# A new table of planner thresholds for the exponential-bound attention stage of an adaLN transformer block

## The chip, the cores and the metric

The kernel runs on one core of a Trainium2 chip. The metric is the device time of one execution in microseconds (us); the median of the runs is compared. Engines are named PE (TensorE matmuls; PEld are its weight loads), DVE (VectorE), ACT (ScalarE), POOL (GpSimd) and SP (SyncE, which issues most transfers).

## The reference

One transformer block with adaptive layer norm, batch 1, 2048 tokens, width 640, in bf16. Six vectors of 640 come from the conditioning row `c`; then attention with 32 heads of 20 and a gated feed-forward layer of width 1536 without an activation.

```python
mod = (silu(c) @ w_mod)                       # six vectors: sa, ca, ga, sb, cb, gb
h = layernorm(x) * (1 + ca) + sa
q, k, v = split(h @ wqkv)                     # 32 heads, 20 wide
p = softmax(q @ k.T * 20 ** -0.5)             # 32 x 2048 x 2048 exponentials
x = x + ga * ((p @ v) @ wo)
h = layernorm(x) * (1 + cb) + sb
x = x + gb * (((h @ w_gate) * (h @ w_up)) @ w_down)
```

## The kernel before

**Units.** Queries are cut into seven chunks (one of 512, six of 256); heads go in eight groups of four, one head on each 32-row strip of PE's array. An item is a chunk and a group. Its work is cut into units: one strip, key tiles of 128 rows, 512 columns of scores in one PSUM bank. For most units PE computes scores (line 1824), ACT takes the exponential of two units at once, 128 x 1024, from PSUM into two of the 16 slots of `PP` (line 2801, 798 instructions), and PE multiplies by the values (PV, line 2504), which frees the slots. 452 units, in 113 groups of four, take another way: DVE turns scores into integers (line 1851), splits them into two factors (lines 1887 and 1895), and multiplies one of them (line 1892 on DVE, or four pieces on POOL, line 1907); both factors then go through PV.

**Work around it.** The rest of the block is cut into rounds ("X work"), one PSUM bank each: transposes of the normalised tiles (line 1390) and their evacuation (lines 1396 and 1398), projections to K, Q and V (lines 1429, 1493 and, with the column-tiled helper, 1233), the output projection, the second layer norm, gate, up and down projections (lines 1233 and 1229). A chunk's output projection and feed-forward layer run while the exponentials of the next chunk go on; what is left of the last two chunks runs after the last exponential, and that is called the tail here. The tiles `hprodt` belong to the last chunk but one, `hprodc` to the last.

**The planner.** The order on each engine is not written by hand. While the program is built, a planner (`Sched`) steps through a modelled time, and at each step gives every free engine its next task; the lists that come out are the instruction order of the engines, which run them strictly in order and wait on semaphores. PE's choice is made in `pick_pe`: scores first when a bank pair is free (`visit`), then X work or PV by thresholds.

The thresholds are module globals. `stage(it)` sets them from a base, then from `STAGE[it]` for the item whose PV is under way, then from `SEGT[segment]`, where a segment is `SEG = 8` exponentials:

```python
    def stage(it):
        globals().update(base)
        globals().update(STAGE.get(it, {}))
        globals().update(SEGT.get(seg[0], {}))

    def segment():
        while sc.progress >= SEG * (seg[0] + 1):
            seg[0] += 1
            stage(st_pv["item"])
```

`sc.progress` counts the exponentials and ends at 798, so segments run from 0 to 99. Segment 0 holds from the first instruction on.

What the thresholds do:

- `XG`: X rounds have a gate, a number of exponentials; a round may start when its gate is not over `progress + XG`.
- `XFIRST`: X work is taken ahead of PV while at least so many pairs of `PP` slots are free. `XCONT`: the same for a round that has been begun.
- `PVMIN`, `PVMAX`, `PVCAP`, `PVTOL`: how many PV units must be ready, how many are taken at once, how late the next scores may get for them. `PV_OPEN`, `PV_KEEP`: how many items PV may be open in, and how many banks it must leave free.
- `HOLD`: PE waits for scores that are so many ns away. `X_HALF`, `X_LATE`: when a matmul of a round is cut in two to let scores in.
- `EAGER`, `D_LATE`, `D_RES`: how early or late scores for the DVE way are made, and when a bank is kept for them.
- `LKTOL`: how long a DVE instruction may be kept waiting by POOL's products. `XBACK`: how many of POOL's pieces may be outstanding when DVE takes a product itself.
- `STEAL_GAP`: ACT takes over an evacuation from DVE when nothing of its own is due within so many ns. In `steal` this ends at 66.2 us of planned time, and begins again only past the last exponential.
- `TPRIO`, `XDPRIO`: priorities, read when the tasks of the DVE way are created, which is before the first call of `stage`.

Of the kernel before, what the change touches and what calls it, by code (L numbers as in the profile page):

```python
# [775 lines left out]

SEG = 8
SEGT = {
    1: {"PVTOL": 152.9, "XFIRST": 5},
    2: {"EAGER": 5},  # L780
    3: {"LKTOL": 409.9, "PVMAX": 4},
    5: {"HOLD": 18.3, "X_HALF": 186.9},
    6: {"PVCAP": 10, "PVTOL": 128.9, "XCONT": 2, "XDPRIO": 1.229},
# [5 lines left out]
    13: {"HOLD": 90.7, "XG": 9},
    14: {"PV_OPEN": 1, "XBACK": 2, "XCONT": 6, "XG": -2},  # L790
    16: {"EAGER": 11, "PVTOL": 31.8, "XCONT": 4},
    17: {"D_RES": 22, "PVTOL": 373.5, "STEAL_GAP": 131.6},
    18: {"D_RES": 22, "LKTOL": 422.8, "PVMAX": 8, "PVMIN": 7, "PVTOL": 373.5, "STEAL_GAP": 131.6},
    20: {"PVTOL": 309.1, "XCONT": 0, "XG": 9},
    21: {"HOLD": 53.2, "PVMIN": 3, "PVTOL": 86.9},
    22: {"D_RES": 49, "PVCAP": 6},
    24: {"HOLD": 52.6},
    25: {"D_LATE": 13, "PV_KEEP": 3},
    26: {"EAGER": 12, "STEAL_GAP": 219.1, "XCONT": 5},
    27: {"XBACK": 2, "XG": -5},  # L800
    28: {"XCONT": 4},
    29: {"D_RES": 18, "EAGER": 15, "HOLD": 1.1, "XFIRST": 2},
    31: {"PVMAX": 6, "XDPRIO": 0.985},
    33: {"XCONT": 2, "XG": 3},
    34: {"HOLD": 14.4, "PVTOL": 187.4},
    36: {"D_LATE": 18, "EAGER": 8, "TPRIO": 0.426},
    37: {"D_LATE": 18, "EAGER": 8, "TPRIO": 0.426, "XCONT": 3},
    38: {"D_LATE": 18, "EAGER": 8, "HOLD": 14.3, "LKTOL": 40.3, "TPRIO": 0.723, "XCONT": 3, "XG": 4},
    39: {"D_LATE": 18, "EAGER": 8, "LKTOL": 40.3, "PV_OPEN": 3, "TPRIO": 0.723, "XCONT": 3, "XG": 4},
    40: {"EAGER": 6, "PVMIN": 6},  # L810
    41: {"EAGER": 3, "XFIRST": 3},
    42: {"EAGER": 4, "PV_OPEN": 1},
    43: {"XG": 14, "X_LATE": 69.8},
    44: {"EAGER": 14, "XFIRST": 5},
    45: {"EAGER": 14, "XFIRST": 5},
    46: {"D_LATE": 22, "D_RES": 20, "HOLD": 148.8},
    47: {"D_LATE": 22, "HOLD": 148.8, "PVMAX": 3, "XG": -2},
    48: {"EAGER": 2},
    49: {"EAGER": 5, "PVCAP": 15, "PV_KEEP": 4, "X_LATE": -212.0},
    50: {"EAGER": 11, "LKTOL": 38.6, "PVCAP": 15, "PV_KEEP": 4, "XDPRIO": 0.893, "X_LATE": -212.0},  # L820
    51: {"PVMIN": 5, "XBACK": 3, "XDPRIO": 0.768},
    52: {"HOLD": 97.6, "PV_OPEN": 3},
    53: {"XBACK": 2},
    54: {"HOLD": 148.1},
    55: {"PVMAX": 9, "PVMIN": 7, "PVTOL": 138.0, "TPRIO": 0.846},
    56: {"HOLD": 2.5, "PVMAX": 9, "PVMIN": 7, "PVTOL": 138.0, "PV_OPEN": 3, "TPRIO": 0.846, "X_HALF": 88.4, "X_LATE": -103.8},
    57: {"HOLD": 2.5, "PVMAX": 9, "PVMIN": 7, "PVTOL": 138.0, "PV_OPEN": 3, "TPRIO": 0.846, "X_HALF": 88.4, "X_LATE": -103.8},
    58: {"HOLD": 59.0},
    59: {"PVMAX": 4, "PV_KEEP": 1},
    60: {"PVCAP": 9, "XCONT": 2},  # L830
    61: {"LKTOL": 659.0, "PV_KEEP": 2},
    62: {"HOLD": 161.6, "XDPRIO": 1.236, "X_LATE": 20.3},
    64: {"PVCAP": 11, "PVMIN": 7, "XG": 10},
    65: {"EAGER": 10, "PVMIN": 3, "TPRIO": 0.795},
    66: {"HOLD": 0, "X_HALF": 144.4},
    67: {"EAGER": 14, "PVMAX": 13, "PV_KEEP": 2},
    68: {"EAGER": 5, "PVMAX": 13, "PV_KEEP": 2, "XG": -6, "X_LATE": 52.7},
    69: {"X_LATE": 187.0},
    70: {"HOLD": 9.6, "X_HALF": 37.7},
    72: {"HOLD": 202.6, "PV_OPEN": 3, "XDPRIO": 1.458},  # L840
    74: {"PVMIN": 5, "PV_KEEP": 4, "XG": 6},
    75: {"EAGER": 6, "HOLD": 0, "PVMIN": 2},
    76: {"LKTOL": 45.1, "PVMIN": 5, "PVTOL": 121.2},
    77: {"LKTOL": 45.1, "PVMIN": 5, "PVTOL": 121.2},
    81: {"X_LATE": 207.1},
    82: {"D_LATE": 37, "EAGER": 13, "XDPRIO": 0.618, "XFIRST": 2, "X_LATE": 207.1},
    83: {"XDPRIO": 1.036, "XFIRST": 4},
    84: {"STEAL_GAP": 206.3, "XCONT": 5},
    85: {"D_LATE": 5, "LKTOL": 647.8, "PV_KEEP": 4, "STEAL_GAP": 206.3, "XCONT": 5, "XG": 11},
    86: {"PVTOL": 117.5, "XBACK": 1, "XCONT": 2, "XFIRST": 4},  # L850
    87: {"PVMIN": 3, "PVTOL": 378.0, "XBACK": 0, "XCONT": 4},
    88: {"HOLD": 193.8},
    89: {"EAGER": 4, "HOLD": 193.8, "PVCAP": 17, "XG": -4},
    91: {"PVMIN": 3, "PV_KEEP": 2, "X_HALF": 0.7},
    93: {"PVCAP": 7, "PVMAX": 9, "X_LATE": -4.5},
    94: {"HOLD": 60.0, "PVCAP": 15, "PVMAX": 9, "X_LATE": -4.5},
    95: {"HOLD": 197.8, "PVCAP": 15, "PVMAX": 5, "PV_KEEP": 1, "X_LATE": -4.5},
    96: {"HOLD": 197.8, "PVCAP": 15, "PVMAX": 5, "PV_KEEP": 1, "XCONT": 5, "X_LATE": -4.5},
# [2214 lines left out]
```

## Time and profile before

| what | value |
|---|---|
| median of 3 runs | 795.71 us (795.64 to 795.74) |
| the profiled execution | 795.55 us, span 793.8 us |
| granted TensorE clock in the profile | 1.000 |
| busy in the span | PE 783.9, ACT 752.4, DVE 711.2, POOL 358.1 us |
| exponentials | 798, from 16.74 us to 762.01 us |

Times in the profile count from the start of the span. Busy time of PE is modelled and overlaps, and an ACT instruction is recorded from its start to its last write, so that neighbours overlap; what an engine waited for tells more than its share. A row of the timeline gives start, length, engine, line, operation, tiles, shapes and count, and in brackets the idle time before it with what ended it. A row of the waits gives the waiting engine and line, the one waited for, the sum in us, the times and the longest.

### The profile page before, as it was taken

How to read it: one execution, taken by the hardware profiler on the slowest of the kernel's cores; microseconds unless marked ns; L12 is line 12 of the kernel's file. 1: busy time of each engine (PE TensorE's matmuls, PEld its weight loads, DVE VectorE, ACT ScalarE, POOL GpSimd, SP SyncE). 2: the span in 40 equal slices, each digit the busy share in tenths (PEclk: the TensorE clock that was granted, in tenths of full speed). 3: DMA queues.
4: the chain of work that ended last, by engine and by line, in shares of the span. 5: the costliest groups of instructions: out<-in, count | busy, mean ns of one | idle time of the engine just before them, and what ended most of it. 6: DMA issues, size and time to landing. Idle time of an engine off the chain costs nothing.

```text
span 793.8 us, 36358 instructions
## 1 busy us (share of the span) xinstructions
PE 783.9 (99%) x16556; PEld 378.9 (48%) x16556; DVE 711.2 (90%) x1317; ACT 752.4 (95%) x837; POOL 358.1 (45%) x372
## 2 busy tenths in 40 slices
PE   8999999999999999999999999999999999999998
PEld 4433433333244444445455555545554455545567
DVE  7889888988999999989999989988999999898974
ACT  6999899999999999999999999999999999999941
POOL 3334646142466555444453536336355445353510
PEclk9999999999999999999999999999999999999999
DMA  9633222102351622110033305131430146214600
GB/s 301 218 111 98 63 61 61 60 25 71 107 130 43 198 46 52 44 36 20 11 94 69 70 19 117 40 68 36 102 86 21 33 105 135 62 38 91 137 20 19
DMA packets 146090, 61.88 MB, mean 78 GB/s; under 512 B 113215, under 2 KB 145935, under 8 KB 145935
## 3 DMA queue, kind: packets, MB, share of 16 engines
q1 hardware_dynamic: 145007, 58.40, 28.5%
q8 instruction: 130, 2.13, 1.1%
q10 hardware_dynamic: 928, 1.15, 0.4%
q14 instruction: 25, 0.20, 0.1%
HBM read 50.53 MB, written 8.99 MB: 75 GB/s over the span
## 4 chain that ended last, share of the span: by engine, by line
ACT 63%; PE 33%; DVE 3%; DMA 0%; issue 0%; SPq 0%
ACT PP L2801 63%; PE ps_all L1824 10%; PE ps_all L1233 8%; PE ps_all L2504 7%; PE ps_all L1493 3%; PE ps_all L1229 3%; DVE DB L1851 1%; DMA x<-in_A_x_dram 0%; PE ps_all L1429 0%; ACT xn L1300 0%; PE ps_all L1390 0%; PE ps_all L2148 0%; DVE DSS L1887 0%; PE ps_all L2966 0%; DVE st L2106 0%
## 5 line engine op out<-in xcount | busy, mean ns | idle before, releaser
L2801 ACT ACTIVATE PP<-ps_all 128x1024 bf16<-128x1024 f32 x798 | 734.6, 1169 | 4.8 <-PE ps_all L2504 2.6
L1907 POOL TENSOR_TENSOR DSS<-DB,DSS 128x512 bf16<-128x512 bf16 x252 | 287.0, 1159 | 309.3 <-DVE DSS L1895 227.1
L1851 DVE TENSOR_SCALAR DB<-ps_all 128x512 int16<-128x512 f32 x452 | 301.9, 683 | 40.3 <-PE ps_all L1824 38.4
L1824 PE MATMUL ps_all<-QT,KT 32*128 32x256 bf16 (+2 forms) x3648 | 315.3, 286 | 3.0 <-ACT PP L2801 1.0
L1824 PEld LDWEIGHTS ps_all<-QT,KT 32*128 32x128 bf16 x3648 | 92.2, 92 | 203.7 <-ACT PP L2801 182.5
L2504 PE MATMUL ps_all<-PP,Vf 128*32 128x256 bf16 (+4 forms) x2844 | 157.6, 290 | 0.3 <-DVE Vf L1593 0.2
L1233 PE MATMUL ps_all<-h2T,stg 128*32 128x256 bf16 (+2 forms) x2784 | 119.6, 279 | 0.2 <-DVE DB L1851 0.2
L2504 PE MATMUL ps_all<-DSS,Vf 128*32 128x256 bf16 (+1 forms) x1608 | 93.3, 288 | 0.1
L2504 PEld LDWEIGHTS ps_all<-PP,Vf 128*32 128x32 bf16 (+1 forms) x2844 | 58.6, 95 | 65.3 <-issue 56.7
L1887 DVE TENSOR_SCALAR DSS<-DB 128x2048 int16<-128x2048 int16 x113 | 79.2, 701 | 0.7
L1895 DVE TENSOR_SCALAR DSS<-DB 128x2048 int16<-128x2048 int16 x113 | 78.3, 693 | 1.2 <-PE ps_all L2504 1.2
L1233 PEld LDWEIGHTS ps_all<-h2T,stg 128*32 128x32 bf16 x2784 | 59.1, 96 | 36.3 <-issue 30.6
L1233 PE MATMUL ps_all<-wd,hprod 128*32 128x320 bf16 (+1 forms) x1364 | 62.3, 280 | 0.2
L1892 DVE TENSOR_TENSOR DSS<-DB,DSS 128x2048 bf16<-128x2048 bf16 x50 | 61.8, 1238 | 0.1
L2504 PEld LDWEIGHTS ps_all<-DSS,Vf 128*32 128x32 bf16 (+1 forms) x1608 | 40.5, 96 | 16.7 <-issue 9.0
L1989 POOL TENSOR_TENSOR OTn<-OT,invT 128x160 bf16<-128x160 f32 (+1 forms) x44 | 26.5, 622 | 44.3 <-DVE invT L1984 44.3
L1233 PEld LDWEIGHTS ps_all<-wd,hprod 128*32 128x32 bf16 x1364 | 31.0, 96 | 15.1 <-issue 11.4
L1233 PE MATMUL ps_all<-wV,hT 128*32 128x160 bf16 x1280 | 36.1, 234 | 0.0
L1493 PE MATMUL ps_all<-hT,wk 128*32 128x512 bf16 (+1 forms) x360 | 32.4, 382 | 0.0
L1493 PE MATMUL ps_all<-hT,wq 128*32 128x512 bf16 x375 | 31.3, 383 | 0.0
L1233 PE MATMUL ps_all<-wo,Ocp 128*32 128x320 bf16 (+1 forms) x656 | 30.2, 282 | 0.3 <-DVE DB L1851 0.2
L1233 PEld LDWEIGHTS ps_all<-wV,hT 128*32 128x32 bf16 x1280 | 23.4, 96 | 13.0 <-issue 8.3
(128 smaller groups left out, 513.8 us busy)
## 6 DMA issues: line engine op xcount, KB each, us to landing
stg<-in_B_w_gate_dram SPq DMA_DIRECT2D x74, 160.0 KB, 2.5
stg<-in_B_w_up_dram SPq DMA_DIRECT2D x74, 160.0 KB, 2.8
KT<-k_rows SPq DMA_DIRECT2D x28, 128.0 KB
QT<-q_rows SPq DMA_DIRECT2D x48, 64.0 KB, 2.1
wm<-in_w_mod_dram SPq DMA_DIRECT2D x3, 800.0 KB, 6.2
x<-in_A_x_dram SPq DMA_DIRECT2D x7, 320.0 KB
k_rows<-KPA SPq DMA_DIRECT2D x16, 128.0 KB, 2.7
wd<-in_B_w_down_dram SPq DMA_DIRECT2D x1, 1920.0 KB
```

The costliest lines, as they stand in the source:

```text
L1229: return lambda e, b: e.matmul(ps[:, b, c0:c0 + n], lhs(), rhs(), start=st, stop=sp)
L1233: return lambda e, b: e.matmul(ps[32 * x:32 * x + 32, b, c0 + o:c0 + o + w], lhs()[:, 32 * x:32 * x + 32], rhs() if w == n else rhs()[:, o ...
L1493: f = [lambda e, b_, k=k, x=x: e.matmul(ps[x:x + min(32, w - x), b_, :], wx[:, k, r0 + x:r0 + min(x + 32, w)], hT[tc][:, k, :], tile_posit ...
L1824: ems.append(lambda e, i=i, kt=kt: e.matmul(dstf()[:, i * u.n:(i + 1) * u.n], KT[32 * u.s:32 * u.s + 32, u.j, kt * 128:(kt + 1) * 128], QT ...
L1851: return e.tensor_scalar(DBl[st_["slot"]][:, x * 512:(x + 1) * 512], bank(cell["b"]), EBIAS, 0.0, op0=ALU.add, op1=ALU.max)
L1887: return e.tensor_scalar(DSl[st_["ss"][0]][:, :], DBl[st_["slot"]][:, :], 0x7F, 0x3F00, op0=ALU.bitwise_and, op1=ALU.bitwise_or)
L1892: return e.tensor_tensor(d, DBl[st_["slot"]][:, :].bitcast(BF16), d, ALU.mult)
L1895: return e.tensor_scalar(DSl[st_["ss"][1]][:, :], DBl[st_["slot"]][:, :], 0x7F80, 2, op0=ALU.bitwise_and, op1=ALU.bitwise_or)
L1907: return e.tensor_tensor(d, DBl[st_["slot"]][:, x * w:x * w + w].bitcast(BF16), d, ALU.mult)
L1989: return lambda e: e.tensor_tensor(OTn[:, g0:g0 + gn, DH * (j + x):DH * (j + x) + DH, :].rearrange("p b c r -> p b r c"), OT[:, nq_ * x:nq ...
L2504: ems.append(lambda e, i=i, kt=kt, stt=stt, stp=stp: e.matmul(ps[32 * s:32 * s + mc, binfo["bank"], c0:c0 + u.n], Vf[:, (kt * H + 4 * u.j ...
L2801: return e.activation(o, ps[:, b0:b0 + nu, :], AFT.Exp, scale=ESCALE)
```

## The change

All entries of `SEGT` are replaced. The functions, the stage table, the base values and the work to be done stay as they are, so the instructions are the same kinds in another order on each engine's list; an evacuation may change between DVE and ACT, a product between DVE and POOL. The old table has 83 entries between segments 1 and 99, the new one has one for each segment from 0 to 100. Cut to the first segments and a few later ones:

```diff
 SEGT = {
-    1: {"PVTOL": 152.9, "XFIRST": 5},
-    2: {"EAGER": 5},
-    3: {"LKTOL": 409.9, "PVMAX": 4},
-    5: {"HOLD": 18.3, "X_HALF": 186.9},
-    6: {"PVCAP": 10, "PVTOL": 128.9, "XCONT": 2, "XDPRIO": 1.229},
-    7: {"D_LATE": 18, "D_RES": 15, "HOLD": 49.8, "PVCAP": 18},
-    9: {"HOLD": 75.5, "XBACK": 2},
-    10: {"EAGER": 14, "HOLD": 75.5, "TPRIO": 0.516, "XBACK": 0},
-    11: {"EAGER": 11, "PVTOL": 20.3, "XCONT": 3, "XG": -8},
...
-    97: {"PVMAX": 10},
-    98: {"X_LATE": -11.0},
-    99: {"PVMAX": 3, "XCONT": 3, "X_HALF": 4.5},
+    0: {"D_LATE": 16, "EAGER": 13, "STEAL_GAP": 188.8, "XG": 12},
+    1: {"D_LATE": 16, "EAGER": 1, "PVMAX": 7, "PVMIN": 7, "STEAL_GAP": 188.8, "XG": 12, "X_HALF": 129.4},
+    2: {"EAGER": 2, "PVCAP": 11},
+    3: {"EAGER": 2, "HOLD": 0, "PVCAP": 11},
+    4: {"EAGER": 2, "PVCAP": 11, "PVMAX": 11, "STEAL_GAP": 187.3, "XFIRST": 2},
+    5: {"EAGER": 2, "HOLD": 127.5, "LKTOL": 736.9, "PVCAP": 11, "PVMAX": 11, "STEAL_GAP": 187.3, "XFIRST": 2},
+    6: {"D_LATE": 23, "PVCAP": 6, "XCONT": 2},
+    7: {"D_LATE": 23, "PVCAP": 6, "XFIRST": 3},
+    8: {"D_LATE": 23, "PVCAP": 6, "PV_OPEN": 2, "XFIRST": 3, "X_LATE": 54.3},
+    9: {"HOLD": 4.3, "PV_OPEN": 1, "STEAL_GAP": 199.2},
+    10: {"LKTOL": 704.1, "PV_KEEP": 4, "XCONT": 3},
+    11: {"D_RES": 60, "PVCAP": 13, "PVTOL": 181.6, "PV_KEEP": 4, "XCONT": 3},
...
+    97: {"D_LATE": 40, "HOLD": 0},
+    98: {"PV_KEEP": 1},
+    99: {"EAGER": 10, "PVCAP": 10, "PVMIN": 3, "XFIRST": 3},
+    100: {"D_LATE": 12, "EAGER": 10, "LKTOL": 106.2, "PVCAP": 10, "PVMIN": 3, "XFIRST": 3, "X_LATE": 159.4},
 }
```

Stage 0, which holds with segment 0, has `"STEAL_GAP": 83.514`; the base value of `XG` and of `XFIRST` is 0.

More of the change, by code (lines that the diff above doesn't have):

```diff
@@ L778 @@
 SEGT = {
-    1: {"PVTOL": 152.9, "XFIRST": 5},
-    2: {"EAGER": 5},
-    3: {"LKTOL": 409.9, "PVMAX": 4},
-    5: {"HOLD": 18.3, "X_HALF": 186.9},
-    6: {"PVCAP": 10, "PVTOL": 128.9, "XCONT": 2, "XDPRIO": 1.229},
-    7: {"D_LATE": 18, "D_RES": 15, "HOLD": 49.8, "PVCAP": 18},
-    9: {"HOLD": 75.5, "XBACK": 2},
-    10: {"EAGER": 14, "HOLD": 75.5, "TPRIO": 0.516, "XBACK": 0},
-    11: {"EAGER": 11, "PVTOL": 20.3, "XCONT": 3, "XG": -8},
-    12: {"EAGER": 6, "PVTOL": 25.5, "XDPRIO": 1.926},
@@ L789 @@
[L789 to L858, printed above, removed]
@@ new lines @@
+    6: {"D_LATE": 23, "PVCAP": 6, "XCONT": 2},
[4 more added lines that the diff above has]
+    11: {"D_RES": 60, "PVCAP": 13, "PVTOL": 181.6, "PV_KEEP": 4, "XCONT": 3},
+    12: {"PVMAX": 4, "PV_OPEN": 3, "X_HALF": 148.6},
+    13: {"PVTOL": 12.4, "XBACK": 0, "XFIRST": 0},
+    14: {"PVTOL": 12.4, "XBACK": 0, "XCONT": 3, "XFIRST": 0},
@@ new lines @@
+    15: {"EAGER": 11},
+    16: {"XCONT": 4},
+    17: {"EAGER": 6, "HOLD": 0, "PV_KEEP": 1, "XFIRST": 6},
+    18: {"D_LATE": 37, "EAGER": 6, "HOLD": 0, "PV_KEEP": 1, "XCONT": 6, "XFIRST": 6},
+    19: {"D_LATE": 16, "XG": -7},
+    20: {"X_LATE": 190.1},
+    21: {"D_LATE": 31, "PVMIN": 2, "X_LATE": 43.2},
+    22: {"D_LATE": 31, "PVCAP": 6, "PVMIN": 2, "X_LATE": 43.2},
+    23: {"HOLD": 114.5},
+    24: {"PVMIN": 7, "PV_OPEN": 2, "XG": -1, "X_LATE": -155.2},
+    25: {"PVMAX": 5},
+    26: {"D_RES": 23, "LKTOL": 416.7, "XFIRST": 6, "X_HALF": 187.2},
@@ new lines @@
+    27: {"EAGER": 2, "XCONT": 0, "XG": 11},
+    28: {"PVMIN": 7},
+    29: {"PVCAP": 5, "PVMIN": 7},
+    30: {"PVCAP": 5, "PVMIN": 7, "XBACK": 0, "XFIRST": 2},
+    31: {"HOLD": 0, "PVCAP": 5, "PVMIN": 7, "XBACK": 0, "XFIRST": 2, "X_HALF": 0},
+    32: {"D_RES": 43, "XCONT": 3},
+    33: {"PVCAP": 5, "XCONT": 7, "X_HALF": 46.2},
+    34: {"PVCAP": 5, "XCONT": 2, "X_HALF": 46.2},
+    35: {"HOLD": 77.2, "PVTOL": 293.3},
+    36: {"X_LATE": 223},
+    37: {"EAGER": 7, "PVCAP": 14, "PV_KEEP": 3, "STEAL_GAP": 43},
@@ new lines @@
+    38: {"PVMIN": 7},
+    39: {"PVMIN": 6, "X_HALF": 105.7},
+    40: {"EAGER": 16, "XFIRST": 6, "X_LATE": 184.1},
+    41: {"PV_KEEP": 2, "XG": 2, "X_HALF": 107.4},
+    42: {"HOLD": 0, "LKTOL": 335.1, "XCONT": 4},
+    43: {"EAGER": 12, "HOLD": 0, "LKTOL": 335.1, "XCONT": 4},
+    44: {"HOLD": 0, "XFIRST": 6},
+    45: {"HOLD": 200.5, "PVMIN": 7, "XG": -2},
+    46: {"HOLD": 63.7, "PVMAX": 13, "PVMIN": 7, "PVTOL": 185.4, "STEAL_GAP": 22.7, "XG": -2},
+    47: {"XG": 4},
+    48: {"PVMAX": 3, "XFIRST": 4, "XG": -3},
@@ new lines @@
+    49: {"PVTOL": 50.4},
+    50: {"X_HALF": 87.8},
+    51: {"PVMIN": 4, "XCONT": 5, "XG": 12},
+    52: {"PVTOL": 371.2, "PV_KEEP": 2, "XCONT": 4},
+    53: {"PVCAP": 11, "X_LATE": 21.6},
+    54: {"LKTOL": 739.9, "PVMIN": 6, "XFIRST": 0},
+    55: {"LKTOL": 739.9, "PVMIN": 6, "XFIRST": 2},
+    56: {"LKTOL": 739.9, "PVMIN": 6, "PVTOL": 330.9, "XCONT": 0, "XFIRST": 4},
+    57: {"PV_OPEN": 1, "XG": 13},
+    58: {"PVMAX": 7, "PVMIN": 6},
+    59: {"EAGER": 15, "PV_KEEP": 2, "STEAL_GAP": 53.4},
@@ new lines @@
+    60: {"EAGER": 15, "PV_KEEP": 2, "STEAL_GAP": 53.4, "XCONT": 0},
+    61: {"HOLD": 115.6, "PVMAX": 3},
+    62: {"D_RES": 21, "EAGER": 2, "HOLD": 0},
+    63: {"LKTOL": 695.8, "XCONT": 5},
+    64: {"PVCAP": 15, "PV_KEEP": 2, "X_LATE": -22.1},
+    65: {"PVCAP": 15, "PVMAX": 2, "PVMIN": 1, "PV_KEEP": 2, "X_LATE": -22.1},
+    66: {"D_RES": 33, "XFIRST": 5},
+    67: {"HOLD": 94.3, "LKTOL": 8.3, "PV_OPEN": 3, "XG": 13},
+    68: {"PVTOL": 121.8, "PV_KEEP": 2},
+    69: {"D_LATE": 26, "PVCAP": 5, "X_LATE": -228.8},
@@ new lines @@
+    70: {"EAGER": 16, "STEAL_GAP": 0},
+    71: {"EAGER": 16, "STEAL_GAP": 0, "XFIRST": 3, "X_LATE": -97.6},
+    72: {"D_LATE": 17, "EAGER": 16, "PV_OPEN": 1, "STEAL_GAP": 0, "XFIRST": 3, "X_HALF": 76.8, "X_LATE": -97.6},
+    73: {"D_LATE": 17, "EAGER": 16, "PVMAX": 2, "PV_OPEN": 1, "STEAL_GAP": 0, "XFIRST": 0, "X_HALF": 76.8, "X_LATE": -97.6},
+    74: {"EAGER": 6, "HOLD": 40.1, "X_LATE": 77.7},
+    75: {"LKTOL": 30.4, "XCONT": 3},
+    76: {"PV_OPEN": 3, "STEAL_GAP": 0},
+    77: {"PVMAX": 2, "STEAL_GAP": 19.5, "XCONT": 7},
@@ new lines @@
+    78: {"EAGER": 3, "XCONT": 3},
+    79: {"EAGER": 3, "HOLD": 90.6, "XCONT": 7},
+    80: {"PV_KEEP": 4, "XFIRST": 6, "X_LATE": -104.5},
+    81: {"EAGER": 6, "PV_KEEP": 4, "STEAL_GAP": 5.3, "X_LATE": -104.5},
+    82: {"EAGER": 11, "PVCAP": 10, "PV_OPEN": 3, "XCONT": 6},
+    83: {"XCONT": 6, "X_LATE": -223.3},
+    84: {"PVTOL": 177.6},
+    85: {"HOLD": 203.7, "PVMAX": 7, "PVTOL": 177.6, "XBACK": 1},
+    86: {"PV_OPEN": 1, "X_LATE": 136.6},
+    87: {"XCONT": 4},
+    88: {"D_LATE": 4, "PVCAP": 19, "X_HALF": 106.8, "X_LATE": -29.9},
@@ new lines @@
+    89: {"X_HALF": 8},
+    90: {"D_LATE": 9, "EAGER": 5, "STEAL_GAP": 43.9, "X_HALF": 8},
+    91: {"PV_OPEN": 3, "X_LATE": 136.5},
+    92: {"XBACK": 2, "XFIRST": 6},
+    93: {"XCONT": 0, "X_LATE": -34.4},
+    94: {"EAGER": 14, "XCONT": 0, "X_LATE": -34.4},
+    95: {"D_RES": 38, "EAGER": 14, "XCONT": 0, "X_LATE": 150.7},
+    96: {"EAGER": 4, "X_HALF": 138.5},
+    97: {"D_LATE": 40, "HOLD": 0},
+    98: {"PV_KEEP": 1},
+    99: {"EAGER": 10, "PVCAP": 10, "PVMIN": 3, "XFIRST": 3},
+    100: {"D_LATE": 12, "EAGER": 10, "LKTOL": 106.2, "PVCAP": 10, "PVMIN": 3, "XFIRST": 3, "X_LATE": 159.4},
```

## The prediction

> **What bounds the kernel now.** I read the page first: busy shares and the chain that ended last.
>
> ```profile
> span 793.8 us, 36358 instructions
> PE 783.9 (99%) x16556; PEld 378.9 (48%) x16556; DVE 711.2 (90%) x1317; ACT 752.4 (95%) x837; POOL 358.1 (45%) x372
> ...
> ACT 63%; PE 33%; DVE 3%; DMA 0%; issue 0%; SPq 0%
> ...
> L2801 ACT ACTIVATE PP<-ps_all 128x1024 bf16<-128x1024 f32 x798 | 734.6, 1169 | 4.8 <-PE ps_all L2504 2.6
> L1907 POOL TENSOR_TENSOR DSS<-DB,DSS 128x512 bf16<-128x512 bf16 x252 | 287.0, 1159 | 309.3 <-DVE DSS L1895 227.1
> L1892 DVE TENSOR_TENSOR DSS<-DB,DSS 128x2048 bf16<-128x2048 bf16 x50 | 61.8, 1238 | 0.1
> ```
>
> PE looks fuller than ACT, so the waits decide which of them waits for the other.
>
> ```profile
> PEld ps_all L1824 <- ACT PP L2801: 182.5, 667, 0.5
> ...
> ACT PP L2801 <- PE ps_all L2504: 2.6, 3, 1.9
> ...
> ACT PP L2801 <- PE ps_all L1824: 1.7, 6, 0.6
> ```
>
> The weight loads ahead of scores waited 182.5 us for exponentials to free their PSUM banks, in 667 waits; the exponentials waited 4.3 us for PE. ACT sets the pace from the first exponential to the last. What stands between the exponentials is in ACT's timeline, in three windows (the second starts where the 81st is running).
>
> ```profile
> 16.74 7.40 ACT L2801 ACTIVATE PP<-ps_all 128x1024 bf16<-128x1024 f32 x8
> 24.23 0.59 ACT L1503 CAST KPA<-ps_all 128x512 bf16<-128x512 f32 x1
> 25.31 0.59 ACT L1443 CAST KT<-ps_all 128x512 bf16<-128x512 f32 x1 [0.49 <-PE ps_all L1429]
> 25.79 0.50 ACT L1594 CAST Vf<-ps_all 128x160 bf16<-128x160 f32 x2
> 26.53 7.44 ACT L2801 ACTIVATE PP<-ps_all 128x1024 bf16<-128x1024 f32 x8 [0.23 <-PE ps_all L1824]
> 33.83 2.29 ACT L1396 ACTIVATE hT<-ps_all,mcol 128x512 bf16<-128x512 bf16 x3
> 36.98 0.78 ACT L1396 ACTIVATE hT<-ps_all,mcol 128x512 bf16<-128x512 bf16 x1 [0.86 <-PE ps_all L1390]
> 37.84 42.27 ACT L2801 ACTIVATE PP<-ps_all 128x1024 bf16<-128x1024 f32 x46
> 80.28 6.52 ACT L2801 ACTIVATE PP<-ps_all 128x1024 bf16<-128x1024 f32 x7 [0.16 <-PE ps_all L1824]
> 88.67 1.94 ACT L2801 ACTIVATE PP<-ps_all 128x1024 bf16<-128x1024 f32 x2 [1.87 <-PE ps_all L2504]
> ...
> 99.64 144.45 ACT L2801 ACTIVATE PP<-ps_all 128x1024 bf16<-128x1024 f32 x157
> 244.27 88.18 ACT L2801 ACTIVATE PP<-ps_all 128x1024 bf16<-128x1024 f32 x95 [0.18 <-PE ps_all L1824]
> 333.05 88.11 ACT L2801 ACTIVATE PP<-ps_all 128x1024 bf16<-128x1024 f32 x96 [0.59 <-PE ps_all L1824]
> ...
> 754.32 7.69 ACT L2801 ACTIVATE PP<-ps_all 128x1024 bf16<-128x1024 f32 x8
> ```
>
> The time falls into three parts: 16.74 us up to the first exponential, 745.27 us from there to the end of the last (754.32 + 7.69 = 762.01), and 31.8 us of tail. One exponential is recorded with 1169 ns on the mean, but they overlap. Eight of them in 7.44 us make (7.44 - 1.17) / 7 = 0.90 us from start to start, and I take that as the floor: 797 x 0.90 + 1.17 = 718.5 us. So 745.3 - 718.5 = 26.8 us lie above the floor, and only an order can move those. The first 80 exponentials took 99.64 - 16.74 = 82.9 us, 10.9 over 80 x 0.90; the other 718 took 662.4 us, or (662.4 - 1.17) / 717 = 0.922 each, 15.9 over.
>
> The Trainium skill, "ScalarE: Activation LUTs", section "What ACT_TABLE_LOAD costs", prices an ACTIVATE with immediate scale and bias at 186 ns plus 0.833 ns an element, less about 93 ns of overlap when they follow back to back. By it, 1024 columns would come every 186 + 853 - 93 = 946 ns, the stretch could not be under 755 us, and no order could win anything in it; this trace's 745.27 us disagrees, and the measurement decides.
>
> **The change, part by part.** Every instruction that does the model's work stays: 798 exponentials, 113 groups on the VectorE route (50 second products on VectorE, 252 / 4 = 63 on GpSimd). The planner reads other thresholds from the start on, so the order differs on every queue. What may change its engine is an evacuation taken over by ACT, and a second product: 1238 ns of VectorE or 4 x 1159 ns of GpSimd, which is 45% busy; this lies beside the exponentials and I price it at nothing as long as the 16 slots of PP do not fill up. Loads on SyncE's queue move with the staging buffers that PE frees; I price that at nothing while other rounds lie between a load and its use. Without that cover a load that lands late would hold PE, which runs its list in order, and with it the scores behind: a block like that in (c).
>
> Some entries cannot act. The counter does not reach segment 100. ACT takes work over only before 66 us or past the last exponential, so STEAL_GAP of segments 9 to 90 is dead. TPRIO and XDPRIO, which the old table sets, were read when tasks were made, before any segment.
>
> (a) *Up to the first exponential, segment 0.* The old table has no segment 0. STEAL_GAP rises from the stage's 83.514 to 188.8 and XG from 0 to 12. Nothing shown excludes either sign; a block of 0.86 us of filler matmuls lies on the chain here.
>
> ```profile
> 10.62 1.12 PE ps_all L1390 x20
> 11.74 0.86 PE ps_all L2994 x4
> 12.61 1.29 PE ps_all L1429 x20
> ```
>
> I bound it by one such block each way, -0.9 to +0.9, and take 0: the fillers stand where normalised tiles are awaited.
>
> (b) *Exponentials 9 and 17, segments 0 to 2.* Between the first eight and the ninth lie 26.53 - 24.14 = 2.39 us, before the seventeenth 37.84 - 33.97 = 3.87: evacuations on ACT, and waits for PE. The ninth needs the second key tile, the seventeenth the third, so some of this stays in any order. The larger STEAL_GAP lets ACT take over less, but the same 0.6 to 0.8 us then falls on VectorE. Ends: -1.6, the three waits of 0.49, 0.23 and 0.86; +1.4, two more evacuations at 0.6 to 0.8. I take -0.3.
>
> (c) *The block at 80 to 91 us, segments 8 and 9.* The exponential at 88.67 waited 1.87 us for L2504, a PV matmul: PP was full, and PV could not drain it. All-engine timeline of that place:
>
> ```profile
> 87.21 0.53 PE L1233 MATMUL ps_all<-wV,hT 128*32 128x160 bf16 x20
> ...
> 87.57 0.85 PE L1233 MATMUL ps_all<-wmb,SCb 128*32 128x320 bf16 x20
> 87.80 0.33 DVE L1593 CAST Vf<-ps_all 128x160 bf16<-128x160 f32 x1
> 88.17 0.10 PEld L2504 LDWEIGHTS ps_all<-PP,Vf 128*32 128x32 bf16 x3
> ```
>
> A V projection, its evacuation at 87.80, and PV right after: PV waited for values, which came late among the projections. The new table brings such work forward ahead of this place (XG 12 in segments 0 and 1; XFIRST 2 in 4 and 5, 3 in 7 and 8, which takes projections before PV while that many pairs of slots are free); the old one has XFIRST only in segment 1, at 5. Ends: -1.9, the whole wait; +1.9, a second of the same kind, since XFIRST also holds PV back. I take -1.2, nearer the gain.
>
> (d) *The other 718 exponentials, segments 10 to 99.* No single wait exceeds 0.6 us. Were all as in the quiet row of 96, (88.11 - 1.17) / 95 = 0.915, the gain would be 717 x 0.007 = 5.0; as in the row of 95, 0.926, the loss 2.9. Most of this is scattered, 0.18 us for eight, in both rows. I take -0.4.
>
> (e) *The tail.* PE ends it, and part of its work there could have come earlier. The window past the last exponential for line 1233 alone (length, then PE's busy time with its count, then the weight loads'), and rows of the chain:
>
> ```profile
> 762.00:793.80 31.80, 4.76 (x124) 3.04 (x124) 1.00 0.07 23
> ...
> 764.26 1.09 PE ps_all L1233 x28
> ...
> 769.17 1.61 PE ps_all L1233 x44
> ...
> 773.34 17.79 PE ps_all L1229 x261
> ```
>
> 124 down-projection matmuls of the chunk before run past the last exponential, 0.038 us each. All done earlier: -4.8.
>
> ```profile
> L1233 PE MATMUL ps_all<-wd,hprodt 128*32 128x320 bf16 x192 | 8.4, 301 | 0.0
> ```
>
> Of that kind there are 192 in all, so 68 were done earlier; all of them late: +2.6. I take -0.3, since in the tail they also stand where PE would wait for the normalisation of the last tile.
>
> Sum: 0 - 0.3 - 1.2 - 0.4 - 0.3 = -2.2 us. The profiled execution took 795.55 us (span 793.8 and 1.75 around it), so 793.35; the median of the runs is 0.16 above it, so 793.5.
>
> **The rivals.** *No change, 795.7.* What the first 80 exponentials gain is given back: the same VectorE work then falls into less time, and VectorE, for which POOL waits above, is nearly full in later stretches.
>
> ```profile
> 230.00:340.00 110.00, 105.84 (x188) 1.00 0.30 79
> 480.00:520.00 40.00, 39.15 (x70) 1.00 0.31 69
> 560.00:660.00 100.00, 96.93 (x168) 1.00 0.29 67
> ```
>
> 96% to 98% here. A backlog ends as full PP slots and one or two waits like (c). Against it: these stretches hold no such wait now. That the new table moves only what is scattered comes to the same time.
>
> *Slower, 798.3.* More of the chunk's down-projections end behind the last exponential: (e) at its upper end, +2.6, with the rest as before. It decides from 1.6 / 0.038 = 42 more matmuls on. For it: thresholds that keep ACT fed defer other work, and its price shows only at the end. Against: PE has slack enough before (the 182.5 us of waits).
>
> *The floor by the skill's rule.* With exponentials at 946 ns nothing in (b), (c) and (d) can be won, and prologue and tail stay: 795.7. As the trace stands 10 us under that floor I leave it 2 in 100.
>
> **How the numbers follow.** Forecast (faster) 48 in 100, no change 28, floor 2, slower 22. A change within 0.2%, 1.6 us, is about what a measurement here cannot tell from none. The range takes half of the summed lower ends of (b) to (e), -13.3 / 2 = -6.6 (they do not fall together), which gives 789.1, and for the upper end the slower case less 0.5, since other parts still gain: 797.8. The forecast's own range is 789.1 to 794.1.
>
> **What would show it.** Right: in ACT's timeline the block near 88 us is gone or under 1 us; the 81st exponential starts before 98.5; the last ends near 760; the tail is 31 to 32 us. (b) wrong: the sum of the two gaps, 6.3 us, moves by over 1.5. (c) wrong: a wait for L2504 of more than 1 us anywhere. (d): the mean over 718 leaves 0.915 to 0.926. (e): the count of 124 moves by over 40. Most of all a new wait of ACT of 2 us or more after 100 us would make the prediction wrong.

## The result and the profile after

The changed kernel takes 788.72 us, median of 4 runs (788.61 to 788.79), beside 795.73 (795.64 to 795.82) before: 7.0 us less, ratio 0.9912 [0.9895, 0.9929]. It is faster, as forecast, but by three times the forecast of 2.2 us; the time lies 0.4 us under the lower end of the range. The profiled execution took 788.79 us. The new table has 18 lines more, so the code behind it stands 18 lines lower: L2819 is the exponential now, L1842 the scores, L2522 PV, L1251 and L1247 the X matmuls. In the kernels of the experiments the same lines have other numbers again; the tiles tell them (`PP<-ps_all` on ACT is the exponential). Five of those kernels ran once each, at a granted clock of 0.996 to 1.000 in the profile, and one execution at a granted clock of 0.852 (830.50 us, of before's order with five moves) is not compared.

The page of the changed kernel:

```profile
span 786.9 us, 36337 instructions
...
PE 776.8 (99%) x16556; PEld 375.7 (48%) x16556; DVE 718.2 (91%) x1327; ACT 750.0 (95%) x836; POOL 318.4 (40%) x336
...
ACT 71%; PE 25%; DVE 3%; DMA 1%; issue 0%; SPq 0%; DVEq 0%
...
L2819 ACT ACTIVATE PP<-ps_all 128x1024 bf16<-128x1024 f32 x798 | 733.5, 1177 | 3.3 <-PE ps_all L1842 1.7
L1925 POOL TENSOR_TENSOR DSS<-DB,DSS 128x512 bf16<-128x512 bf16 x216 | 245.7, 1155 | 321.7 <-DVE DSS L1913 254.9
...
L1910 DVE TENSOR_TENSOR DSS<-DB,DSS 128x2048 bf16<-128x2048 bf16 x59 | 72.7, 1233 | 0.2
```

The matmuls are the same 16556; nine second products went from POOL to DVE (50 to 59, 63 to 216 / 4 = 54). On the chain that ended last PE's share fell from 33% to 25%. The waits, with total, count and longest:

```profile
PEld ps_all L1842 <- ACT PP L2819: 183.8, 681, 0.8
...
ACT PP L2819 <- PE ps_all L1842: 1.7, 4, 0.6
...
ACT PP L2819 <- PE ps_all L2522: 1.0, 1, 1.0
```

The exponentials' waits for PE sum to 2.7 us instead of 4.3. That is 1.6 of 7.0 us: the list of waits alone does not show where the rest went. ACT's timeline does, over the first 80 exponentials and then over the others:

```profile
16.97 7.40 ACT L2819 ACTIVATE PP<-ps_all 128x1024 bf16<-128x1024 f32 x8
...
26.78 7.44 ACT L2819 ACTIVATE PP<-ps_all 128x1024 bf16<-128x1024 f32 x8 [0.23 <-PE ps_all L1842]
35.66 0.59 ACT L1461 CAST KT<-ps_all 128x512 bf16<-128x512 f32 x1 [1.44 <-PE ps_all L1447]
36.88 19.36 ACT L2819 ACTIVATE PP<-ps_all 128x1024 bf16<-128x1024 f32 x21 [0.63 <-PE ps_all L1842]
56.73 4.69 ACT L2819 ACTIVATE PP<-ps_all 128x1024 bf16<-128x1024 f32 x5 [0.50 <-PE ps_all L1842]
61.75 32.78 ACT L2819 ACTIVATE PP<-ps_all 128x1024 bf16<-128x1024 f32 x35 [0.33 <-PE ps_all L1842]
95.50 10.20 ACT L2819 ACTIVATE PP<-ps_all 128x1024 bf16<-128x1024 f32 x11 [0.97 <-PE ps_all L2522]
...
99.14 658.79 ACT L2819 ACTIVATE PP<-ps_all 128x1024 bf16<-128x1024 f32 x717
```

The block of 1.87 us at 88.67 is gone; one of 0.97 stands at 95.50, and two of 0.50 and 0.33 are new. The last row is the largest change to see: 717 exponentials without one break, which means that ACT is nowhere idle for more than 0.15 us between them. The same stretch of before had five breaks, of 0.18 and 0.59 us at 244.27 and 333.05 and these three:

```profile
495.70 91.33 ACT L2801 ACTIVATE PP<-ps_all 128x1024 bf16<-128x1024 f32 x99 [0.29 <-PE ps_all L1824]
587.21 22.11 ACT L2801 ACTIVATE PP<-ps_all 128x1024 bf16<-128x1024 f32 x24 [0.19 <-PE ps_all L1824]
609.74 152.27 ACT L2801 ACTIVATE PP<-ps_all 128x1024 bf16<-128x1024 f32 x166 [0.42 <-PE ps_all L2504]
```

The last exponential ends at 99.14 + 658.79 = 757.93, not 762.01. The tail as a window with each engine's busy time (length; PE, its weight loads, DVE, ACT, POOL; clock and transfers), before:

```profile
762.01:793.80 31.79, 28.74 (x489) 24.45 (x487) 18.25 (x51) 3.31 (x10) 1.10 (x2) 1.00 0.07 23
```

And after, all engines and then the line of the down-projections alone:

```profile
757.93:786.90 28.97, 25.94 (x431) 22.54 (x429) 16.38 (x47) 4.42 (x12) 1.10 (x2) 1.00 0.06 20
...
757.93:786.90 28.97, 2.88 (x76) 1.80 (x76) 1.00 0.06 20
```

PE's idle time in the tail is the same (31.79 - 28.74 = 3.05, 28.97 - 25.94 = 3.03); it has 58 fewer matmuls to do, 48 of them down-projections of the chunk before.

Where the 6.9 us of the span went, from the starts of the exponentials in the two traces:

| part | before | after | change | forecast |
|---|---|---|---|---|
| (a) up to the first exponential | 16.74 | 16.97 | +0.2 | 0 |
| (b) first to 17th start | 21.10 | 19.91 | -1.2 | -0.3 |
| (c) 17th to 81st start | 61.81 | 61.35 | -0.5 | -1.2 |
| (d) 81st start to the last end | 662.37 | 659.70 | -2.7 | -0.4 |
| (e) tail | 31.75 | 28.98 | -2.8 | -0.3 |

Up to the start of the last exponential (d) is -3.0; that exponential is itself recorded with 1.02 us in after and 0.72 in before.

### The profile page after: what moved, and what is told of

It is laid out like the page before. It is cut to its first block, busy times and chain, and to the rows that moved or that the text cites. A ratio compares the mean times of both kernels' runs of the same rounds, so it can differ in the third digit from the quotient of the medians.

```text
span 786.9 us, 36337 instructions
## 1 busy us (share of the span) xinstructions
PE 776.8 (99%) x16556; PEld 375.7 (48%) x16556; DVE 718.2 (91%) x1327; ACT 750.0 (95%) x836; POOL 318.4 (40%) x336
## 4 chain that ended last, share of the span: by engine, by line
ACT 71%; PE 25%; DVE 3%; DMA 1%; issue 0%; SPq 0%; DVEq 0%
ACT PP L2819 71%; PE ps_all L1842 7%; PE ps_all L1251 6%; PE ps_all L2522 5%; PE ps_all L1247 3%; PE ps_all L1511 2%; DVE DB L1869 1%; PE ps_all L1408 1%; DMA x<-in_A_x_dram 1%; PE ps_all L1447 0%; PE ps_all L1272 0%; DVE DSS L1913 0%; ACT xn L1318 0%; DVE DSS L1905 0%; PE ps_all L2166 0%; PE ps_all L3012 0%
## 5 line engine op out<-in xcount | busy, mean ns | idle before, releaser
L2819 ACT ACTIVATE PP<-ps_all 128x1024 bf16<-128x1024 f32 x798 | 733.5, 1177 | 3.3 <-PE ps_all L1842 1.7
L1925 POOL TENSOR_TENSOR DSS<-DB,DSS 128x512 bf16<-128x512 bf16 x216 | 245.7, 1155 | 321.7 <-DVE DSS L1913 254.9
L1842 PE MATMUL ps_all<-QT,KT 32*128 32x256 bf16 (+2 forms) x3648 | 315.1, 286 | 3.9 <-ACT PP L2819 2.5
L1842 PEld LDWEIGHTS ps_all<-QT,KT 32*128 32x128 bf16 x3648 | 92.0, 92 | 202.1 <-ACT PP L2819 183.8
L2522 PE MATMUL ps_all<-PP,Vf 128*32 128x256 bf16 (+3 forms) x2844 | 159.4, 290 | 0.6 <-DVE Vf L1611 0.5
L1251 PE MATMUL ps_all<-h2T,stg 128*32 128x256 bf16 (+2 forms) x2812 | 123.3, 277 | 0.1
L2522 PE MATMUL ps_all<-DSS,Vf 128*32 128x256 bf16 (+3 forms) x1608 | 91.1, 287 | 0.0
L2522 PEld LDWEIGHTS ps_all<-PP,Vf 128*32 128x32 bf16 (+1 forms) x2844 | 55.3, 94 | 68.0 <-issue 60.2
L1251 PEld LDWEIGHTS ps_all<-h2T,stg 128*32 128x32 bf16 x2812 | 60.6, 96 | 33.7 <-issue 27.0
L1910 DVE TENSOR_TENSOR DSS<-DB,DSS 128x2048 bf16<-128x2048 bf16 x59 | 72.7, 1233 | 0.2
L1251 PE MATMUL ps_all<-wd,hprod 128*32 128x320 bf16 (+1 forms) x1364 | 60.8, 281 | 0.0
L2522 PEld LDWEIGHTS ps_all<-DSS,Vf 128*32 128x32 bf16 (+1 forms) x1608 | 40.7, 96 | 13.4 <-issue 8.6
L1251 PE MATMUL ps_all<-wV,hT 128*32 128x160 bf16 x1280 | 38.9, 234 | 0.0
L1251 PEld LDWEIGHTS ps_all<-wd,hprod 128*32 128x32 bf16 x1364 | 29.1, 96 | 17.4 <-issue 13.9
L1251 PEld LDWEIGHTS ps_all<-wV,hT 128*32 128x32 bf16 x1280 | 24.5, 96 | 14.5 <-issue 9.5
L1251 PE MATMUL ps_all<-wo,Ocp 128*32 128x320 bf16 (+1 forms) x640 | 30.4, 285 | 0.1
```

The lines of the kernel that those rows point to most:

```text
L1251: return lambda e, b: e.matmul(ps[32 * x:32 * x + 32, b, c0 + o:c0 + o + w], lhs()[:, 32 * x:32 * x + 32], rhs() if w == n else rhs()[:, o ...
L1842: ems.append(lambda e, i=i, kt=kt: e.matmul(dstf()[:, i * u.n:(i + 1) * u.n], KT[32 * u.s:32 * u.s + 32, u.j, kt * 128:(kt + 1) * 128], QT ...
L1910: return e.tensor_tensor(d, DBl[st_["slot"]][:, :].bitcast(BF16), d, ALU.mult)
L1925: return e.tensor_tensor(d, DBl[st_["slot"]][:, x * w:x * w + w].bitcast(BF16), d, ALU.mult)
L2522: ems.append(lambda e, i=i, kt=kt, stt=stt, stp=stp: e.matmul(ps[32 * s:32 * s + mc, binfo["bank"], c0:c0 + u.n], Vf[:, (kt * H + 4 * u.j ...
L2819: return e.activation(o, ps[:, b0:b0 + nu, :], AFT.Exp, scale=ESCALE)
```

## The experiments

In the quoted expectations, A says that each entry of the table fits only the order that the entries before it made; B, that the entries are rules that help anywhere. C says that the tail follows the number of leftover down-projections, 0.038 us each; D, that it is fixed. For (d), E says that PE has a little room beside each exponential and that what exceeds it is paid; F, that PE's 184 us of waits are room enough; G, that PE has none; H, that work of PE which is moved is paid at another place.

**Is the gain made piece by piece?** The first kernel has the new entries for segments 0 to 41 and the old ones from 42 on; the second has no entries; the third has each new entry one segment later.

```diff
-SEGT = NEW
+SEGT = NEW[0..41] + OLD[42..99]      # first
+SEGT = {}                            # second
+SEGT = {k + 1: NEW[k]}               # third
```

> The new table for segments 0 to 41, the old one from 42 on. Theory A, the entries fit one order and no other: the exponentials up to the 337th start within 0.2 us of the new kernel's (the 81st at 98.2, the 337th at 333.1); after that the old entries meet an order they were not found for, and the rest takes over 5 us longer than in the kernel before, total over 798 us. Theory B, the entries are good or bad rules in themselves: the 3.6 us gained by the 337th exponential stay, the rest runs like the kernel before, total near 792.

> No entry at all in the segment table; the stage table alone. Theory A: what the segment entries win over the stage table is many times the 7 us between the two tables, total over 808 us, with both a longer stretch of exponentials and a longer tail than before. Theory B: the entries are small corrections, total within 8 us of the kernel before, 788 to 804.

> The new table with every entry one segment (eight exponentials) later. Theory A: the same values out of step are worth nothing, total over 808 us, as with no table. Theory B: rules of this kind hold as well eight exponentials later, total within 4 us of the new kernel, 785 to 793.

Measured: 810.26, 829.39 and 826.73 us, beside 795.74 for before. The first follows the new kernel up to the splice (the 337th exponential starts at 332.98, after: 333.06, before: 336.68) and then loses 17 us of the span to it by the last end (775.10). Most of what leaving out the table costs stands in one row of that kernel's waits:

```profile
ACT PP L2718 <- PE ps_all L2421: 25.7, 12, 7.6
```

PP was full twelve times, for up to 7.6 us. This is theory A, and B falls: the same entries that save 7 us against before cost 31 when they are shifted by eight exponentials. The rival "given back" falls too, since in the new kernel nearly all that is gained is kept: the 81st exponential starts 1.4 us earlier than before, the 281st 2.6, the 521st 3.6, the 641st 4.4.

**What moved the 17th exponential?** `XG` is taken out of segment 0, all else stays.

```diff
-    0: {"D_LATE": 16, "EAGER": 13, "STEAL_GAP": 188.8, "XG": 12},
+    0: {"D_LATE": 16, "EAGER": 13, "STEAL_GAP": 188.8},
```

> The new table without XG 12 in segment 0, all else kept. If this entry makes the 1.2 us gained before the 17th exponential, its start falls back from 36.9 to about 38 us, as in the kernel before (37.8), with evacuations of hT on ACT again. Theory A adds that all later entries then miss their order: total over 808 us. Theory B: only about 1.2 us are lost, total near 790.

Measured: 831.00 us. ACT's timeline:

```profile
26.50 7.44 ACT L2819 ACTIVATE PP<-ps_all 128x1024 bf16<-128x1024 f32 x8 [0.23 <-PE ps_all L1842]
33.75 0.84 ACT L1414 ACTIVATE hT<-ps_all,mcol 128x512 bf16<-128x512 bf16 x1
35.09 0.78 ACT L1414 ACTIVATE hT<-ps_all,mcol 128x512 bf16<-128x512 bf16 x1 [0.49 <-PE ps_all L1408]
36.99 0.78 ACT L1414 ACTIVATE hT<-ps_all,mcol 128x512 bf16<-128x512 bf16 x1 [1.12 <-PE ps_all L1408]
37.85 7.44 ACT L2819 ACTIVATE PP<-ps_all 128x1024 bf16<-128x1024 f32 x8
```

The evacuations of the third key tile are back on ACT, as in before, and the 17th exponential starts at 37.85 (before 37.84, after 36.88). In after the transposes of that tile start earlier, at 29.43 us instead of 32.51, and their evacuations begin on DVE while ACT is still in the second eight:

```profile
30.83 0.99 DVE L1416 TENSOR_SCALAR hT<-ps_all,mcol 128x512 bf16<-128x512 bf16 x2
```

ACT is left with one cast there. Without `XG` in segment 0 the stretch from the first to the 17th start takes 21.14 us, as before (21.10), so this entry makes the whole of (b). `STEAL_GAP`, to which the prediction gave it, has no part: built without any of its `STEAL_GAP` entries, the new table makes the same list for every engine. Of the 42 us that are lost in all, 27.7 lie in seven waits for PV and 8.4 in a longer tail (37.4 us): theory A again.

**What moved the block at 88 us?** `XFIRST` is taken out of segment 4.

```diff
-    4: {"EAGER": 2, "PVCAP": 11, "PVMAX": 11, "STEAL_GAP": 187.3, "XFIRST": 2},
+    4: {"EAGER": 2, "PVCAP": 11, "PVMAX": 11, "STEAL_GAP": 187.3},
```

> The new table without XFIRST 2 in segment 4. The prediction's step (c) says that such entries bring projections forward, and that the wait of an exponential for PV between 80 and 96 us (1.0 us in the new kernel, 1.9 before) comes from a late V projection: then the 73rd exponential starts over 1.5 us later than the new kernel's 89.7, and ACT waits over 2 us for PV before 100 us. If XFIRST here does not matter for it, the 73rd starts within 0.5 us of 89.7. By theory A the total is over 808 us in the first case.

Measured: 833.65 us. Three rows of ACT's timeline:

```profile
80.67 3.78 ACT L2819 ACTIVATE PP<-ps_all 128x1024 bf16<-128x1024 f32 x4 [0.48 <-PE ps_all L2522]
85.76 2.85 ACT L2819 ACTIVATE PP<-ps_all 128x1024 bf16<-128x1024 f32 x3 [1.31 <-PE ps_all L1842]
89.86 1.94 ACT L2819 ACTIVATE PP<-ps_all 128x1024 bf16<-128x1024 f32 x2 [1.25 <-PE ps_all L2522]
```

The 17th exponential starts as in after (36.96), the 73rd at 92.87 (after 89.65), and the waits for PV are back, 2.7 us of them up to 100 us. The evacuation of values at 87.80, for which PV waited in before, is the 22nd from the start, and comes when 69 exponentials have started. The 22nd in after, where 66 have started:

```profile
83.19 0.32 DVE L1611 CAST Vf<-ps_all 128x160 bf16<-128x160 f32 x1
```

And without `XFIRST` in segment 4, where 69 have started, as before:

```profile
89.01 0.31 DVE L1611 CAST Vf<-ps_all 128x160 bf16<-128x160 f32 x1
```

So `XFIRST` in segment 4 is needed for (c), with the other entries as they are.

**Does the tail follow the leftover down-projections?** The new table up to segment 87 or 95, the old one behind it.

```diff
-SEGT = NEW
+SEGT = NEW[0..87] + OLD[88..99]      # first
+SEGT = NEW[0..95] + OLD[96..99]      # second
```

> The new table up to segment 87, the old one from 88 on. Up to the 705th exponential it runs like the new kernel (671.2 us, within 0.2). Theory C, the tail is as long as PE's leftover: tail = 29.0 + 0.038 x (down-projection matmuls of the last chunk but one past the last exponential, less 76), within 1 us, and the count is over 76, since these entries did not see this order. Theory D, the last tile's own chain sets the tail: it stays at 29 to 30 us whatever the count.

> The new table up to segment 95, the old one for the last four segments, 30 exponentials. The last exponential ends within 0.6 us of the new kernel's 757.9. Theory C: the tail grows by 0.038 us for each down-projection matmul more than 76. Theory D: the tail stays at 29 to 30 us.

Measured: 792.52 us, 0.9960 [0.9945, 0.9975] of before, and 790.32, 0.9932 [0.9917, 0.9947]. In both the last exponential ends where it does in after, within 0.4 us; only the tail differs. The window past the last exponential for the line of the down-projections, first kernel:

```profile
758.31:790.72 32.41, 6.23 (x156) 3.97 (x156) 1.00 0.07 22
```

The same window in the second kernel:

```profile
757.89:788.50 30.61, 4.30 (x104) 2.53 (x104) 1.00 0.07 23
```

With 156, 104 and 76 leftovers the tail is 32.4, 30.6 and 29.0 us: 3.4 us for 80 matmuls, 0.043 each. The first two have the same 15 matmuls of output projection in the tail, after has 13; between these two alone it is 1.8 us for 52, 0.035 each. Theory C, and D falls. Before, with 124, has 31.75, 0.7 over the line through these. In after the leftovers explain 48 x 0.038 = 1.8 of the 2.8 us. Most of the rest is output projection that after has done before the end. Its group in the tail of before:

```profile
L1229 PE MATMUL ps_all<-wo,Ocp 128*128 128x320 bf16 x19 | 2.9, 299 | 0.1
```

And in the tail of after:

```profile
L1247 PE MATMUL ps_all<-wo,Ocp 128*128 128x320 bf16 x13 | 2.1, 300 | 0.1
```

2.9 us against 2.1; four PV matmuls less make most of the last 0.2.

**Is PE's waiting room to spare?** At 59 places in the stretch of (d), one score task in twelve is issued twice, or three times, into the same banks, where the same values are written again (214 and 428 matmuls more); the expectations say 60 places.

```diff
+    for t in order["pe"]:
+        if <scores, number 80 to 789, every twelfth>:
+            t.emits = t.emits * 2            # or * 3
```

> The new kernel's order, with the score matmuls of every twelfth exponential from the 81st to the 790th issued twice into the same bank (60 places, about 0.3 us of PE each; nothing else changes). PE's stretch from one score pair to the next grows from 0.81 us to about 1.1 there. Theory E, an exponential comes late where that stretch passes about 1.0 us, and by the excess: 60 x 0.1 = 6 us slower, 2 to 9. Theory F, PE's 184 us of waiting for ACT absorb it: under 1 us. Theory G, PE is full and every matmul counts: 60 x 0.3 = 18 us.

> As the run before, with the scores issued three times: about 0.6 us more of PE in 60 places, the stretch about 1.4 us there. Theory E: 60 x 0.4 = 24 us slower than the new kernel, 18 to 28. Theory F: under 3 us. Theory G: 60 x 0.6 = 36 us.

Measured: 794.35 us, 0.9983 [0.9974, 0.9993] of before, and 806.79, 1.0139 [1.0124, 1.0154]: 5.6 and 18.1 us over after's 788.72. The tail stays at 29.0. PE's own time for the scores was 315.1 us; the group on the page of the kernel with two:

```profile
L1845 PE MATMUL ps_all<-QT,KT 32*128 32x256 bf16 (+2 forms) x3862 | 327.1, 286 | 2.2 <-ACT PP L2822 1.4
```

On the page of the kernel with three:

```profile
L1845 PE MATMUL ps_all<-QT,KT 32*128 32x256 bf16 (+2 forms) x4076 | 339.9, 286 | 2.1 <-ACT PP L2822 1.5
```

In the same kernel, the waits of the exponentials for scores (1.7 us in four without doses):

```profile
ACT PP L2822 <- PE ps_all L1845: 8.6, 33, 0.6
```

And two rows of its ACT timeline:

```profile
317.24 11.10 ACT L2822 ACTIVATE PP<-ps_all 128x1024 bf16<-128x1024 f32 x12 [0.18 <-PE ps_all L1845]
328.58 11.21 ACT L2822 ACTIVATE PP<-ps_all 128x1024 bf16<-128x1024 f32 x12 [0.23 <-PE ps_all L1845]
```

The first dose adds 12.0 us to PE, 0.20 a place where 0.3 was expected, and 5.6 to the time; the second 12.8 and 12.4. So (12.0 - 5.6) / 59 = 0.11 us per place were free, and what exceeds it is paid nearly one to one. This is theory E, at the low end of what it expected for the kernel with three; F (under 3) and G (36) fall. In the last two rows ACT breaks off every twelfth exponential, at the doses. A break of 0.2 us costs more than its 0.2: two neighbours that follow at once overlap by 1.17 - 0.90 = 0.27 us on the mean, and part of that is lost too. By the starts, the 29 breaks behind the 81st exponential cost 0.11 to 0.21 us each beyond the idle time shown.

**Is it the place of the scores, or the work around them?** Behind the 81st exponential, before has 34 stretches of over 1.0 us in which PE starts no score matmul, 5.4 us over 1.0 together; after has 24 with 2.4 us (counted from the traces' PE rows). The difference of 3.0 us is as much as (d) gained by the starts. Two more kernels were run: before's order, with the scores of five late exponentials moved ahead of the PV batch in front of them; and after's order with five such moves.

```diff
+    for idx in (237, 332, 509, 595, 608):    # in after: 37, 42, 251, 573, 792
+        s = scores of exponential idx
+        <s goes ahead of the PV units that stand before it on PE's list,
+         not further than the exponential that frees its banks>
```

> The kernel before, with only the score matmuls of five late exponentials (those at 244.3, 333.1, 495.7, 574.9 and 587.2 us, which come 0.32 to 0.73 us late, 2.5 us in sum) moved ahead of the PV batch before them in PE's list. Theory E, the block of PE work between two score pairs makes the lateness: 1.2 to 2.4 us faster than before, the five late by under 0.25 us each. Theory H, PE's work is only moved and the lateness comes back at the next exponentials: within 0.4 us of before.

> The new kernel with the same done at its five late exponentials that have PV ahead of their scores (at 56.7, 61.8, 255.3, 551.3 and 752.2 us, 0.24 to 0.78 us late, 2.4 us in sum). Theory E: 1.0 to 2.3 us faster than the new kernel's 788.7. Theory H: within 0.4 us of it.

Measured: 796.84 us, 1.0012 [1.0003, 1.0021] of before, and 789.16, 0.9917 [0.9903, 0.9930]. PE's timeline at the second place, in before:

```profile
330.88 0.39 PE L1824 MATMUL ps_all<-QT,KT 32*128 32x256 bf16 x4
331.20 0.62 PE L1233 MATMUL ps_all<-h2T,stg 128*32 128x512 bf16 x8
331.64 0.61 PE L2504 MATMUL ps_all<-PP,Vf 128*32 128x256 bf16 x16
332.07 0.61 PE L2504 MATMUL ps_all<-DSS,Vf 128*32 128x256 bf16 x16
332.62 0.60 PE L1824 MATMUL ps_all<-QT,KT 32*128 32x256 bf16 x10
```

With the move:

```profile
332.05 0.39 PE L1837 MATMUL ps_all<-QT,KT 32*128 32x256 bf16 x4
332.38 0.41 PE L2517 MATMUL ps_all<-PP,Vf 128*32 128x256 bf16 x8
332.60 0.62 PE L2517 MATMUL ps_all<-DSS,Vf 128*32 128x256 bf16 x16
333.15 0.40 PE L1837 MATMUL ps_all<-QT,KT 32*128 32x256 bf16 x6
333.48 1.26 PE L1246 MATMUL ps_all<-h2T,stg 128*32 128x512 bf16 x20
334.68 0.39 PE L1837 MATMUL ps_all<-QT,KT 32*128 32x256 bf16 x4
```

And the row of ACT's timeline that follows there:

```profile
335.11 162.42 ACT L2814 ACTIVATE PP<-ps_all 128x1024 bf16<-128x1024 f32 x177 [0.50 <-PE ps_all L1837]
```

In before PE has no scores from 331.27 to 332.62. The move puts a group at 332.05, and that exponential, 0.73 us late in before, is 0.08 late. But the PV that was passed stands behind it now, with 20 X matmuls at 333.48, and the next break comes two exponentials later, 0.50 us at 335.11. At four of the five places it went so, and at the fifth the lateness came back one exponential later. The time is 1.1 us over before's in the same comparison, and in after the five moves cost 0.4 us. So theory E, which expected a gain from these moves, falls; of H the mechanism is what the rows show, but it expected to stay within 0.4 us, and before's order lost more. The lateness lies in how much other work PE has within a few exponentials, not in its order at the spot.

## Why the prediction was right in sign and short in size

- *What bounds it.* "ACT sets the pace from the first exponential to the last" holds for most exponentials only. That PE waited 182.5 us was read as slack, in the argument against the slower rival ("PE has slack enough before"); the doses in after show 0.11 us a place. What was priced at nothing beside the exponentials stayed so: nine second products went to DVE, and after has one wait with PP full, of 0.97 us, and its list of waits has none of PE for a load.
- *(a)* stands: +0.2 us. The seven runs of other kernels that begin with the new order have their first exponential at 16.76 to 17.06, so this is no more than the spread.
- *(b)* is the step with the wrong cause. The sum of the two gaps, 6.3 us, moved to 5.1, by less than the 1.5 that the prediction set as its mark; the -1.2 lies within its ends, but by luck. The prediction expected no gain from evacuations that leave ACT, and a gain only from shorter waits for PE. The reverse happened: before the 17th exponential four evacuations of hT (3.1 us) gave way to one cast (0.6), and the waits there grew from 0.86 to 2.07 us. And it put the move down to `STEAL_GAP`; `XG` in segment 0 did it, which the prediction named in (a) and counted in (c).
- *(c)* is right in kind (`XFIRST` brings values forward, the block is under 1 us) and too large: 0.97 us of waiting stands at 95.50 and 0.83 at two new places, where before had 1.87 at 88.67 and two waits of 0.16 and 0.30. The 81st exponential starts at 98.23, before the 98.5 that was named. (b) and (c) together were given -1.5 and made -1.7.
- *(d)* is the first mis-sized term, -0.4 against -2.7. Its mean left 0.922 for 0.9185, inside the band of 0.915 to 0.926 that was set. The step that failed is the size taken from "Most of this is scattered". As a description that holds: 63 exponentials of before start 0.95 us or more behind their neighbour and 62 of after, and those without a break cost 7.5 and 7.2 us over a spacing of 0.904. But the part that is not scattered, the five breaks between the long rows, cost 2.8 us (1.67 us of idle time and 0.14 to 0.44 us more at each), and none of them is in after. They stood in the timeline; two of them (0.18 and 0.59) were quoted, and passed over as "No single wait exceeds 0.6 us".
- *(e)* is the other, -0.3 against -2.8. The price per matmul was right (0.038, and 0.035 to 0.043 by the runs), the count moved by 48, over the 40 that was set as the mark. The step that failed is the reason for taking a value near nothing, that in the tail these matmuls stand where PE would wait for the normalisation: PE's idle time there is 3.0 us with 124 of them and with 76, and so each matmul less shortens the tail.
- *The range* took half of the summed lower ends since "they do not fall together". (d) and (e) did fall together, each by a little over half of its end, and the measured time came out below the range.
- *The floor.* The trace runs under the 946 ns again: 717 exponentials in (658.79 - 1.17) / 716 = 0.918 us each. The Trainium skill has a second figure, in "Perfetto Trace Analysis", section "Optimizing Scalar/DVE Operations": about 51 ns a ScalarE instruction on PSUM. With the 0.833 ns an element of the Trainium skill's "ScalarE: Activation LUTs", section "What ACT_TABLE_LOAD costs", that makes an estimate of 853 + 51 = 904 ns for 1024 columns read from PSUM. The traces agree: 0.904 us is the commonest spacing from start to start behind the 81st exponential, in before and in after.

Open: which entries removed the five breaks. By theory A no single one can be put into the old table for a test, since all that follows changes with it; it was not tried. In before four of the five end with scores and one, at 609.74, with PV. So for (d) the runs show how a break of the first kind comes about (too much other work of PE around the score matmuls), and not what in the table took the five away.

## What to carry to other kernels

An engine that waits often on the pacing engine is not thereby spare: the test is a small dose of extra work, and here 0.11 us was free at each dosed place. Price a break in a back-to-back stream as its idle time plus the overlap that it destroys (0.1 to 0.4 us here), and count the breaks between long rows of the timeline before calling a loss scattered. A threshold of such a planner is worth what it is only in the order that the entries before it made: one early entry taken out cost 42 us and another 45, while the old entries for the last 12 and the last 4 segments cost 3.8 and 1.6.

## What the runs showed that was not expected

One threshold at the start moved the end by 42 us (831.00 against 788.72), and a shift of the whole table by one segment by 38, with the same work to do: over half of the loss comes as a few waits with PP full (27.7 us in seven and 23.3 us in nine, up to 9.7 us each). And where matmuls were added, PE's busy share did not tell of them: 99% on the page of after, and 99% with the scores issued two and three times, where PE's busy time went from 776.8 to 784.4 and 797.0 us and its idle time from 10.1 to 8.1 and 8.0.
